# Layer 2 of a fused attention and two-layer kernel as seven products of halved operands

## The chip, the cores and the metric

The kernel runs on one core of a Trainium2 chip. The metric is the device time of one execution in microseconds, the median of the runs shown. The engines are named as in the profile: PE (TensorE, matrix products), PEld (its weight loads), DVE (VectorE), ACT (ScalarE), POOL (GpSimd) and SP (SyncE, which only issues transfers here).

## The reference

Eight batches of 8 heads, 576 positions and 64 features go through causal attention, where heads 0 to 3 see the last 32 positions ("local") and heads 4 to 7 the positions of the same residue modulo 32 ("strided"). The result, 4608 tokens by 512, goes through two layers:

```python
x = attn_out.transpose(0, 2, 1, 3).reshape(B * S, H * D)   # 4608 x 512
h = x @ w_in                                               # 4608 x 2048
g = np.maximum(h, 0.0) + alpha * np.minimum(h, 0.0)
return g @ w_out                                           # 4608 x 512
```

## The kernel before

The 4608 tokens of the two layers are nine chunks of 512. A chunk is two stages on PE, with attention for a later batch laid between their pieces.

**Layer 1** (`lin1_piece`, lines 614 to 639): 16 pieces, one for each block m of 128 columns of d_ff. A piece is four matmuls of 512 moving columns (line 624, `win16` stationary, `xT` moving) into one PSUM buffer `hps`. ACT then forms `neg` = relu(-h) (line 634), and DVE forms g = neg * (1 - alpha, negated) + h in f16 (line 637) into `gTs[n][:, m, :]`. The DVE instruction is put on a list, `late`, and issued in the next attention step, behind the instructions of that step's piece (lines 600 to 609).

**Layer 2** (`lin2_piece`, lines 643 to 671): for each of four groups of 128 tokens, four pieces of four matmuls (line 665) with a block of g as the stationary operand and 512 columns of `wout16` moving. The sixteen matmuls of a group add up in one PSUM buffer `ops`; ACT copies it to `osb` (line 670), and SP stores it (line 671). The last group of the last chunk is made in two halves of 256 columns (lines 650 to 663), so that the last store is short.

The PSUM buffers of layer 1, layer 2 and, in chunk 0, of some scores come from one pool of three (`phpool`); a buffer is given out again when its reader is done. A second pool of three (`pspool`) serves transposes, the second half of the scores and the pv products. `gT` has two buffers, `osb` three.

**Attention** is cut into pieces, in a list written out by hand (lines 537 to 592): scores of a pair of heads (PE, then exp on ACT, then the mask multiplication on POOL, lines 414 and 421), pv products (PE line 442, then a reciprocal and a multiplication on DVE, lines 449 and 451), transposes of q and k (line 239, evacuated by DVE and ACT), and the transposition of x into `xT`, on PE or by a transfer. `xT` is a ring of four batches of 576 tokens (line 50); batch b lies at (b % 4) * 576, and a chunk that runs over the end of the ring has its layer-1 matmuls split in two.

**The order.** Every engine runs its instructions in the order in which the code issues them (`keep`). The loop at lines 790 to 806 goes over chunks 1 to 8 and, in each, over 32 pieces, 16 of layer 1 and 16 of layer 2; behind each piece it issues as many attention steps as a running account gives (line 801), so that the pieces of one batch are spread over the chunk. Chunk 0 has its own loops (lines 778 to 785). POOL's queue also holds casts (`cast_copy`, line 183) and the issues of many loads (lines 114 to 171), in the same order as the pieces that they belong to. Batches 2 to 7 are computed beside chunks 1 to 6; chunks 7 and 8 have no attention beside them.

Of the kernel before, what the change touches and what calls it, by code (L numbers as in the profile page):

```python
# [31 lines left out]
def kernel(  # L32
# [24 lines left out]
    hpool = ctx.enter_context(tc.tile_pool(name="half", bufs=4))  # L57
    xpool = ctx.enter_context(tc.tile_pool(name="xp", bufs=3))
    rpool = ctx.enter_context(tc.tile_pool(name="rp", bufs=4))
    gpool = ctx.enter_context(tc.tile_pool(name="gp", bufs=2))  # L60
    npool = ctx.enter_context(tc.tile_pool(name="np", bufs=3))
    opool = ctx.enter_context(tc.tile_pool(name="op", bufs=3))
    pspool = ctx.enter_context(tc.tile_pool(name="ps", bufs=3, space=bass.MemoryType.PSUM))
    phpool = ctx.enter_context(tc.tile_pool(name="ph", bufs=3, space=bass.MemoryType.PSUM))
    pbpool = ctx.enter_context(tc.tile_pool(name="pb", bufs=1, space=bass.MemoryType.PSUM))
# [390 lines left out]
    def x_piece(P):  # L456
        xp = pspool.tile([128, 1024], F16, tag="ps", name="xp")
        for t in range(P.n):
            keep(nc.tensor.transpose(  # L459
                xp[:, P.w * t : P.w * t + P.w], P.x16[0 : P.w, 128 * t : 128 * t + 128], ident[0 : P.w, 0 : P.w]))  # L460
        base = (P.b % 4) * S
        if P.strided:
            keep(nc.scalar.copy(  # L463
                xT[:, P.hp, base : base + S].rearrange("r (p t) -> r p t", t=8),
                xp[:, 0:576].rearrange("r (t p) -> r p t", t=8)))
        else:
            cast_copy("act" if P.b < NEARLY and P.hp == 0 else "dve",
                      xT[:, P.hp, base : base + S], xp[:, 0:576])

    def x_dma(P):  # L470
        base = (P.b % 4) * S
        if P.strided:
            P.xs = xpool.tile([128, 8, 80], F16, tag="xs", bufs=2, name="xs")
            keep(nc.sync.dma_start_transpose(P.xs, P.x16[0:80, :]))
        else:
            keep(nc.sync.dma_start_transpose(
                xT[:, P.hp, base : base + S].rearrange("r (w p) -> r w p", p=96), P.x16[0:96, 0:768]))

    def x_copy(P):
        base = (P.b % 4) * S  # L480
# [116 lines left out]

        return max(i for i, (g, _) in enumerate(pieces) if g == 4 * b + 3) + 1

    late = []  # L600

    def attn_step(end):
        if pos["i"] < end:
            pieces[pos["i"]][1]()
            pos["i"] += 1
        while late:
            late.pop(0)()
        if defer:
            defer.pop(0)()


    gTs = {}

    def lin1_piece(n, m):
        if m == 0:
            gTs[n] = gpool.tile([128, 16, 512], F16, tag="gT", name="gT")
        c0 = (512 * n) % RING
        parts = [(c0, 0, min(512, RING - c0))]
        if c0 + 512 > RING:
            parts.append((0, RING - c0, 512 - (RING - c0)))  # L620
        hps = phpool.tile([128, 512], F32, tag="hps", name="hps")
        for kk in range(4):
            for x, (src, dst, w) in enumerate(parts):
                keep(nc.tensor.matmul(  # L624
                    hps[:, dst : dst + w],
                    win16[:, kk, 128 * m : 128 * m + 128],
                    xT[:, kk, src : src + w],
                    start=(kk == 0 and x == 0),
                    stop=(kk == 3 and x == len(parts) - 1),
                    skip_group_check=True,  # L630
                ))

        neg = npool.tile([128, 512], F32, tag="neg", name="neg")
        keep(nc.scalar.activation(neg, hps, AF.Relu, scale=-1.0))  # L634

        def fin():
            keep(nc.vector.scalar_tensor_tensor(  # L637
                gTs[n][:, m, :], neg, oma[:, m : m + 1], hps, op0=ALU.mult, op1=ALU.add))
        late.append(fin)

    ops_cur = {}

    def lin2_piece(n, i):
        mt, part = i // 4, i % 4
        last = n == NCH - 1
        if part == 0:
            ops_cur["t"] = phpool.tile([128, 512], F32, tag="hps", name="ops")
        ops = ops_cur["t"]
        r0 = 512 * n + 128 * mt
        if last and mt == 3:  # L650

            if part in (1, 3):
                return
            c0 = 128 * part
            half = phpool.tile([128, 512], F32, tag="hps", name="ops3") if part else ops
            for kf in range(16):
                keep(nc.tensor.matmul(  # L657
                    half[:, 0:256], gTs[n][:, kf, 128 * mt : 128 * mt + 128],
                    wout16[:, kf, c0 : c0 + 256], start=(kf == 0), stop=(kf == 15)))
            osb = opool.tile([128, 512], F32, tag="osb", name="osb")  # L660
            keep(nc.vector.tensor_copy(osb[:, 0:256], half[:, 0:256]))
            keep(nc.sync.dma_start(out[r0 : r0 + 128, c0 : c0 + 256], osb[:, 0:256]))
            return
        for kf in range(4 * part, 4 * part + 4):
            keep(nc.tensor.matmul(  # L665
                ops, gTs[n][:, kf, 128 * mt : 128 * mt + 128], wout16[:, kf, :],
                start=(kf == 0), stop=(kf == 15)))
# [169 lines left out]
```

## Time and profile before

| | |
|---|---|
| median of 3 runs | 325.08 us (324.74 to 327.92) |
| span of the profiled execution, first to last instruction | 321.1 us |
| PE, DVE, ACT, POOL busy | 312.0, 180.8, 173.0, 144.0 us |
| mean granted TensorE clock | 1.000 |
| chunk 1, from the stretch 63.9 to 99.7 | 35.8 us |
| chunk 5, from the stretch 198.5 to 231.4 | 32.9 us |
| chunk 7, from the stretch 262.2 to 289.8 | 27.6 us |

The time of the profiled execution itself is not listed beside its span; the median lies 4.0 us above the span. A profile's "busy" counts an engine as busy while an instruction runs; matmuls are pipelined, so the time that one takes from PE is read from the distance of the next one, not from its own duration. In the groups the figures after the bar are busy time in us, mean ns of one, then the idle time of the engine before them with what ended it.

### The profile page before, as it was taken

The page shows a single profiled execution, that of the slowest core. Times are in us where ns is not written, and L with a number is a line of the kernel's source. Part 1 is how long each engine was busy: PE and PEld are TensorE (multiplying, and loading weights), DVE is VectorE, ACT ScalarE, POOL GpSimd, SP SyncE. Part 2 cuts the span into 40 slices and gives each one's busy share as a digit, 9 for nine tenths or more (in the row PEclk, how much of TensorE's full clock was granted, in tenths as well). Part 3 has the DMA queues.
Part 4 walks back from the last instruction along what each step waited for, and adds up shares of the span by engine and source line. Part 5 has one row for each costly group of instructions (what it writes and reads, how often), then busy time and mean ns, then how long its engine had stood idle before and what let it go on. Part 6 is the DMA issues. An engine that isn't in the chain of part 4 may idle for free.

```text
span 321.1 us, 6319 instructions
## 1 busy us (share of the span) xinstructions
PE 312.0 (97%) x2493; PEld 162.8 (51%) x2493; DVE 180.8 (56%) x354; ACT 173.0 (54%) x322; POOL 144.0 (45%) x154
## 2 busy tenths in 40 slices
PE   6999989999999999999999999999999999999995
PEld 2564456554554454445568754455444544444444
DVE  5576836477554873388338833884288328406801
ACT  1765655368347753774477546754576157416610
POOL 8772489406998445844485338532612200000000
PEclk9999999999999999999999999999999999999999
DMA  7999999995599975997399639972611220020011
GB/s 235 194 206 207 228 174 176 182 270 159 105 141 200 200 81 127 199 149 97 91 182 202 93 88 167 84 94 62 141 51 20 61 94 2 0 98 35 0 65 65
DMA packets 77597, 40.33 MB, mean 126 GB/s; under 512 B 58480, under 2 KB 69248, under 8 KB 77568
## 3 DMA queue, kind: packets, MB, share of 16 engines
q0 software_dynamic: 41728, 17.38, 46.5%
q1 hardware_dynamic: 35840, 22.55, 29.4%
q8 instruction: 19, 0.31, 0.4%
q14 instruction: 10, 0.08, 0.1%
HBM read 38.01 MB, written 9.44 MB: 148 GB/s over the span
## 4 chain that ended last, share of the span: by engine, by line
PE 88%; DMA 4%; DVE 2%; ACT 2%; POOL 2%; issue 1%; SPq 0%; DVEq 0%; ACTq 0%
PE hps L624 38%; PE ops L665 36%; PE pv L442 4%; PE tp L239 2%; DMA xs<-x16s 2%; DMA kl<-in_k_dram 2%; PE wps L687 2%; PE sp L399 1%; PE xp L459 1%; PE ops L657 1%; ACT qT L179 1%; PE sph L399 1%; DVE qT L181 1%; POOL vs L183 1%; DVE x L451 1%
## 5 line engine op out<-in xcount | busy, mean ns | idle before, releaser
L637 DVE SCALAR_TENSOR_TENSOR gT<-neg,oma,hps 128x512 f16<-128x512 f32 x144 | 106.1, 744 | 53.1 <-ACT neg L634 45.0
L665 PE MATMUL ops<-wout,gT 128*128 128x512 f16 x560 | 135.3, 379 | 0.0
L624 PE MATMUL hps<-xT,win 128*128 128x512 f16 (+1 forms) x640 | 132.6, 358 | 0.5
L634 ACT ACTIVATE neg<-hps 128x512 f32<-128x512 f32 x144 | 86.1, 598 | 38.8 <-PE hps L624 38.8
L624 PEld LDWEIGHTS <-win 128*128 128x128 f16 x640 | 60.2, 98 | 59.4 <-issue 3.0
L665 PEld LDWEIGHTS <-gT 128*128 128x128 f16 x560 | 49.1, 98 | 47.1
L414 POOL TENSOR_TENSOR et<-et,consts 128x576 f16<-128x576 f16 (+1 forms) x24 | 30.6, 1275 | 82.1 <-ACT et L412 77.9
L670 ACT COPY osb<-ops 128x512 f32<-128x512 f32 x35 | 20.5, 586 | 66.3 <-PE ops L665 66.0
L449 DVE RECIPROCAL rc<-pv 72x6 f32<-72x6 f32 (+2 forms) x80 | 14.9, 186 | 53.5 <-PE pv L442 53.1
L451 DVE TENSOR_TENSOR x<-pv,rc 96x384 f16<-96x384 f32 (+2 forms) x62 | 33.0, 532 | 2.1
L442 PEld LDWEIGHTS <-et 72*128 72x128 f16 (+1 forms) x448 | 24.2, 98 | 16.9 <-POOL et L421 0.9
L421 POOL TENSOR_TENSOR et<-et,consts 128x576 f16<-128x576 f16 (+1 forms) x24 | 30.5, 1270 | 2.6 <-ACT et L418 2.4
L412 ACT ACTIVATE et<-sp 128x576 f16<-128x576 f32 (+1 forms) x24 | 15.5, 646 | 10.4 <-PE sp L399 10.4
L418 ACT ACTIVATE et<-sph 128x288 f16<-128x288 f32 (+1 forms) x48 | 18.6, 408 | 0.0
L687 PE MATMUL wps<-wrm 128*128 128x512 f16 x44 | 15.7, 431 | 1.2 <-DVE wrm L699 1.2
L442 PE MATMUL pv<-vs,et 72*128 72x65 f16 x256 | 15.5, 193 | 0.0
L183 POOL COPY vs<-stv 72x1024 f16<-72x1024 f16 x14 | 14.3, 1032 | 0.0
L171 POOL DMA_DIRECT2D vl<-in_v_dram x8 | 11.3, 1410 | 5.1 <-PE pv L442 4.0
L399 PEld LDWEIGHTS <-kT 64*128 64x128 f16 x336 | 7.1, 95 | 9.9 <-issue 8.9
L442 PE MATMUL pv<-vl,et 128*128 128x65 f16 x192 | 11.1, 194 | 0.4 <-POOL et L421 0.4
L181 DVE COPY qT<-tp 128x1024 f16<-128x1024 f16 (+1 forms) x9 | 9.4, 1045 | 3.3 <-PE tp L239 3.3
L463 ACT COPY xT<-xp 128x576 f16<-128x576 f16 x10 | 6.4, 639 | 6.8 <-PE xp L459 6.8
(88 smaller groups left out, 201.1 us busy)
## 6 DMA issues: line engine op xcount, KB each, us to landing
out_dram<-osb SPq DMA_DIRECT2D x35, 256.0 KB, 2.3
ql<-in_q_dram SPq DMA_DIRECT2D x6, 512.0 KB, 5.1
kl<-in_k_dram SPq DMA_DIRECT2D x6, 512.0 KB, 5.8
stv<-in_v_dram POOLq DMA_DIRECT2D x8, 288.0 KB, 7.2
vl<-in_v_dram POOLq DMA_DIRECT2D x6, 384.0 KB, 7.4
win<-in_moe_w_in_dram POOLq DMA_DIRECT2D x4, 512.0 KB, 9.6
wout<-in_moe_w_out_dram POOLq DMA_DIRECT2D x4, 512.0 KB, 13.4
qsd<-in_q_dram POOLq DMA_DIRECT2D x6, 288.0 KB, 6.9
```

Source lines behind the costliest of these rows:

```text
L183: keep(nc.gpsimd.tensor_copy(o, i))
L414: keep(nc.gpsimd.tensor_tensor(mv, mv, m, op=ALU.mult))
L418: keep(nc.scalar.activation(ev[:, n * y : n * y + n], sps[y][0:r, 0:n], AF.Exp, scale=SCALE))
L421: keep(nc.gpsimd.tensor_tensor(mv, mv, m, op=ALU.mult))
L442: keep(nc.tensor.matmul(pv[:, 65 * x : 65 * x + 65], et[0:r, c : c + 128], v16[0:r, 2 * P.pr + hh, t, :] if P.strided else v16[:, 6 * (2 * ...
L451: keep(nc.vector.tensor_tensor(P.x16[0:w, c0 : c0 + 64 * nb].rearrange("r (c e) -> r c e", e=64), pvv[:, :, 0:64], rc[0:w, 0:nb].unsqueeze ...
L624: keep(nc.tensor.matmul(hps[:, dst : dst + w], win16[:, kk, 128 * m : 128 * m + 128], xT[:, kk, src : src + w], start=(kk == 0 and x == 0) ...
L634: keep(nc.scalar.activation(neg, hps, AF.Relu, scale=-1.0))
L637: keep(nc.vector.scalar_tensor_tensor(gTs[n][:, m, :], neg, oma[:, m : m + 1], hps, op0=ALU.mult, op1=ALU.add))
L665: keep(nc.tensor.matmul(ops, gTs[n][:, kf, 128 * mt : 128 * mt + 128], wout16[:, kf, :], start=(kf == 0), stop=(kf == 15)))
L670: keep(nc.scalar.copy(osb, ops))
L687: keep(nc.tensor.matmul(wps, wrm[:, 0:128], wrm, start=True, stop=True))
```

## The change

For chunks 1 to 8, layer 2 is computed with seven products of halves instead of eight. The tokens of a chunk are two halves of 256 (`lo`, `hi`), the output columns two halves of 256, and the sixteen d_ff blocks two sets of eight, the even and the odd ones. Each product is 2 x 8 matmuls (two groups of 128 tokens, eight blocks) with 256 moving columns, accumulating in one half of a PSUM buffer.

- The products need sums of g, in a new tile `sg`. DVE forms two (`g_sums`) in three parts, behind pieces 7, 13 and 15 of layer 1 (4, 3 and 1 blocks of 256 elements); POOL forms the other two (`g_sums2`), each in two parts of 1024 elements, issued behind pieces 8 and 12 of layer 1 and behind the first and the fifth piece of layer 2.
- They need sums of the weights, made once on DVE: three sums (`wt`) in six instructions of 1024 elements beside layer 2 of chunk 0, and a fourth, in place in `wout16`, in two instructions behind pieces 2 and 5 of chunk 1's layer 1.
- The products are combined partly in PSUM and partly by DVE: five additions of 128x512 from PSUM, and two copies by ACT (P1, P2), take the place of ACT's four copies. Three PSUM buffers X, Y and V hold the products. Each chunk stores four blocks of 256 tokens by 256 columns. In the last chunk, V is two buffers, and its additions and stores are halves.
- `gT` has one buffer instead of two, `osb` five instead of three, and `xT` holds three batches instead of four, so that chunks 3 and 6 run over its end (before: chunk 4).
- `late` is gone: the g instruction is issued directly behind `neg`, ahead of the next attention piece. The 30 pieces of a chunk have their own spread of the attention steps.

```diff
-    RING = 4 * S
+    RING = 3 * S
+    FAST = 1
+    GS = {7: (0, 4), 13: (4, 7), 15: (7, 8)}
...
-    gpool = ctx.enter_context(tc.tile_pool(name="gp", bufs=2))
+    gpool = ctx.enter_context(tc.tile_pool(name="gp", bufs=1))
...
-    opool = ctx.enter_context(tc.tile_pool(name="op", bufs=3))
+    opool = ctx.enter_context(tc.tile_pool(name="op", bufs=5))
...
-        while late:
-            late.pop(0)()
...
-        def fin():
-            keep(nc.vector.scalar_tensor_tensor(
-                gTs[n][:, m, :], neg, oma[:, m : m + 1], hps, op0=ALU.mult, op1=ALU.add))
-        late.append(fin)
+        keep(nc.vector.scalar_tensor_tensor(
+            gTs[n][:, m, :], neg, oma[:, m : m + 1], hps, op0=ALU.mult, op1=ALU.add))
+        if n >= FAST:
+            g_sums(n, m)
...
+    def g_sums(n, m):
+        if m not in GS:
+            return
+        if m == min(GS):
+            sums["t"] = cpool.tile([128, 4, 8, 256], F16, tag="sg", name="sg")
+        a, b = GS[m]
+        st, g = sums["t"], gTs[n].rearrange("r (p j) t -> r j p t", j=2)
+        lo, hi = slice(0, 256), slice(256, 512)
+        P = slice(a, b)
+        sub(nc.vector, st[:, 0, P], g[:, 0, P, hi], g[:, 1, P, hi], ALU.add)
+        sub(nc.vector, st[:, 1, P], st[:, 0, P], g[:, 0, P, lo])
+
+    def g_sums2(n, P, k):
+        ...
+        if k == 2:
+            sub(nc.gpsimd, st[:, 2, P], g[:, 0, P, lo], g[:, 0, P, hi])
+        else:
+            sub(nc.gpsimd, st[:, 3, P], g[:, 1, P, lo], st[:, 1, P])
+
+    def w_sums(k, P):
+        w = wout16.rearrange("r (p j) c -> r j p c", j=2)
+        lo, hi = slice(0, 256), slice(256, 512)
+        o, x, y, op = (
+            (wt[:, 0, P], w[:, 1, P, hi], w[:, 0, P, hi], ALU.subtract),
+            (wt[:, 1, P], wt[:, 0, P], w[:, 0, P, lo], ALU.add),
+            (wt[:, 2, P], w[:, 1, P, lo], wt[:, 1, P], ALU.subtract),
+            (w[:, 0, P, hi], w[:, 0, P, hi], w[:, 0, P, lo], ALU.subtract))[k]
+        sub(nc.vector, o, x, y, op)
+
+    PRODUCTS = ("P1", "P6", "P2", "P7", "P5", "P4", "P3")
+
+    def fast_piece(n, i):
+        name, tb = PRODUCTS[i // 2], i % 2
...
+        bank, x, y = {
+            "P1": ("X", g[:, 0, :, lo], w[:, 0, :, lo]),
+            "P2": ("X", g[:, 1, :, lo], w[:, 1, :, lo]),
+            "P6": ("Y", st[:, 1], wt[:, 1]),
+            "P7": ("Y", st[:, 2], wt[:, 0]),
+            "P4": ("Y", g[:, 1, :, hi], wt[:, 2]),
+            "P5": ("V", st[:, 0], w[:, 0, :, hi]),
+            "P3": ("V", st[:, 3], w[:, 1, :, hi]),
+        }[name]
...
+        for p in range(8):
+            keep(nc.tensor.matmul(
+                z[:, 256 * tb : 256 * tb + 256], x[:, p, 128 * tb : 128 * tb + 128], y[:, p],
+                start=(opens and p == 0 and (tb == 0 or own)), stop=(ends and p == 7),
+                skip_group_check=True))
+        if tb == 0 and not own:
+            return
...
+        if name == "P1":
+            keep(nc.scalar.copy(new("21"), z))
+        elif name == "P6":
+            sub(nc.vector, new("12"), z, cur["21"], ALU.add)
+        elif name == "P2":
+            keep(nc.scalar.copy(new("11"), z))
+            store(0, 0, cur["11"])
+        elif name == "P7":
+            sub(nc.vector, new("22"), z, cur["21"], ALU.add)
+        elif name == "P5":
+            sub(nc.vector, cur["22"][:, c], z[:, c], cur["22"][:, c], ALU.add)
+            store(1, 1, cur["22"], h)
+        elif name == "P4":
+            sub(nc.vector, cur["21"], z, cur["21"], ALU.add)
+            store(1, 0, cur["21"])
+        else:
+            sub(nc.vector, cur["12"][:, c], z[:, c], cur["12"][:, c], ALU.add)
+            store(0, 1, cur["12"], h)
...
     for i in range(16):
         lin2_piece(0, i)
+        if i % 2 and i < 12:
+            w_sums(i // 4, slice(4 * (i // 2 % 2), 4 * (i // 2 % 2) + 4))
...
-        for i in range(32):
+        for i in range(30):
             if i < 16:
                 lin1_piece(n, i)
+                if n == 1 and i in (2, 5):
+                    w_sums(3, slice(0, 4) if i == 2 else slice(4, 8))
+                if i == 8:
+                    g_sums2(n, slice(0, 4), 2)
+                if i == 12:
+                    g_sums2(n, slice(0, 4), 3)
             else:
-                lin2_piece(n, i - 16)
+                fast_piece(n, i - 16)
+                if i == 16:
+                    g_sums2(n, slice(4, 8), 2)
+                if i == 20:
+                    g_sums2(n, slice(4, 8), 3)
             if i >= skip:
-                acc += left / ((21 if n == B - 2 else 22.5) - 0.5 * skip) * (0.5 if i < 16 else 1.0)
+                acc += left / ((20 if n == B - 2 else 21.2) - 0.5 * skip) * (0.5 if i < 16 else 1.0)
```

More of the change, by code (lines that the diff above doesn't have):

```diff
@@ L82 @@
     wout16 = cpool.tile([128, 16, 512], F16)
+    wt = cpool.tile([128, 3, 8, 256], F16)
     xT = cpool.tile([128, 4, RING], F16)
@@ L460, in x_piece @@
                 xp[:, P.w * t : P.w * t + P.w], P.x16[0 : P.w, 128 * t : 128 * t + 128], ident[0 : P.w, 0 : P.w]))
-        base = (P.b % 4) * S
+        base = (P.b % 3) * S
         if P.strided:
@@ L470, in x_dma @@
     def x_dma(P):
-        base = (P.b % 4) * S
+        base = (P.b % 3) * S
         if P.strided:
@@ L479, in x_copy @@
     def x_copy(P):
-        base = (P.b % 4) * S
+        base = (P.b % 3) * S
         keep(nc.scalar.copy(
@@ L598, in attn_until @@
         return max(i for i, (g, _) in enumerate(pieces) if g == 4 * b + 3) + 1
-    late = []
     def attn_step(end):
@@ L634, in lin1_piece, with sub @@
         keep(nc.scalar.activation(neg, hps, AF.Relu, scale=-1.0))
-        def fin():
-            keep(nc.vector.scalar_tensor_tensor(
-                gTs[n][:, m, :], neg, oma[:, m : m + 1], hps, op0=ALU.mult, op1=ALU.add))
-        late.append(fin)
+        keep(nc.vector.scalar_tensor_tensor(
+            gTs[n][:, m, :], neg, oma[:, m : m + 1], hps, op0=ALU.mult, op1=ALU.add))
+        if n >= FAST:
+            g_sums(n, m)
+    sums = {}
+    def sub(eng, o, x, y, op=ALU.subtract):
+        keep(eng.tensor_tensor(o, x, y, op=op))
@@ new lines, in g_sums @@
+    def g_sums(n, m):
[10 more added lines that the diff above has]
+    def g_sums2(n, P, k):
+        st, g = sums["t"], gTs[n].rearrange("r (p j) t -> r j p t", j=2)
+        lo, hi = slice(0, 256), slice(256, 512)
[3 more added lines that the diff above has]
+            sub(nc.gpsimd, st[:, 3, P], g[:, 1, P, lo], st[:, 1, P])
@@ new lines, in w_sums @@
+    def w_sums(k, P):
+        w = wout16.rearrange("r (p j) c -> r j p c", j=2)
+        lo, hi = slice(0, 256), slice(256, 512)
+        o, x, y, op = (
[5 more added lines that the diff above has]
+    PRODUCTS = ("P1", "P6", "P2", "P7", "P5", "P4", "P3")
@@ new lines, with new, store @@
+    cur = {}
+    def fast_piece(n, i):
+        name, tb = PRODUCTS[i // 2], i % 2
+        last = n == NCH - 1
+        g = gTs[n].rearrange("r (p j) t -> r j p t", j=2)
+        w = wout16.rearrange("r (p j) c -> r j p c", j=2)
+        st = sums["t"]
+        lo, hi = slice(0, 256), slice(256, 512)
+        bank, x, y = {
[7 more added lines that the diff above has]
+        }[name]
+        opens = name in ("P1", "P6", "P5")
+        ends = name in ("P2", "P4", "P3")
+        if opens and tb == 0:
+            cur[bank] = [phpool.tile([128, 512], F32, tag="hps", name="f" + bank)] * 2
+            if last and bank == "V":
+                cur[bank] = [cur[bank][0], pspool.tile([128, 512], F32, tag="ps", name="fV1")]
+        z = cur[bank][tb]
+        own = last and bank == "V"
+        for p in range(8):
[5 more added lines that the diff above has]
+            return
+        def new(key):
+            cur[key] = opool.tile([128, 512], F32, tag="osb", name="o" + key)
+            return cur[key]
+        def store(i, k, t, h=slice(0, 2)):
+            r0, m = 512 * n + 256 * i + 128 * h.start, h.stop - h.start
+            keep(nc.sync.dma_start(
+                out[r0 : r0 + 128 * m, 256 * k : 256 * k + 256].rearrange("(b p) c -> p b c", p=128),
+                t[:, 256 * h.start : 256 * h.stop].rearrange("p (b c) -> p b c", c=256)))
+        h = slice(tb, tb + 1) if own else slice(0, 2)
+        c = slice(256 * h.start, 256 * h.stop)
+        if name == "P1":
[16 more added lines that the diff above has]
+            store(0, 1, cur["12"], h)
```

## The prediction

> **What bounds the kernel now.** I read the page first for the share of each engine, then the chain of waits for what sets the end, then the stretches stage by stage, then the groups by shape for prices, and last the timelines of three places that the change touches.
>
> ```profile
> span 321.1 us, 6319 instructions
> ...
> PE 312.0 (97%) x2493; PEld 162.8 (51%) x2493; DVE 180.8 (56%) x354; ACT 173.0 (54%) x322; POOL 144.0 (45%) x154
> ```
>
> PE is busy 97% of the span. Its weight loads (PEld) lie beside its matmuls.
>
> ```profile
> 165.47 2.62 PE hps L624 x24
> ...
> 262.19 13.81 PE hps L624 x64
> 276.00 13.81 PE ops L665 x64
> ...
> 313.99 3.51 PE ops L657 x32
> ```
>
> This is the chain of waits (start, length, what). In chunk 7 PE runs 64 matmuls of 512 columns in 13.81 us, 0.216 each. The 256-column ones, each with its own weight load, take 2.62/24 = 0.109 (chunk 4, where the x ring wraps) and 3.51/32 = 0.110. Half the columns cost half the time, so a product of halves is paid by columns.
>
> ```profile
> core 0: us, PE busy (x) PEld busy (x) DVE busy (x) ACT busy (x) POOL busy (x), PEclk, DMA share, GB/s
> 63.90:99.70 35.80, 35.02 (x315) 17.85 (x314) 21.77 (x42) 22.75 (x44) 24.76 (x24) 1.00 1.00 168
> ...
> 198.50:231.40 32.90, 32.82 (x268) 16.33 (x266) 19.57 (x38) 19.26 (x36) 16.92 (x16) 1.00 0.70 108
> ...
> 262.20:276.00 13.80, 13.80 (x65) 6.25 (x64) 10.65 (x15) 9.62 (x17) 0.00 (x0) 1.00 0.05 20
> ```
>
> The stretches: chunk 1, chunk 5, and layer 1 of chunk 7. DVE's average of 56% hides that it is the near second in layer 1: 10.65 of 13.80 there, for fifteen of the sixteen g instructions.
>
> ```profile
> L637 DVE SCALAR_TENSOR_TENSOR gT<-neg,oma,hps 128x512 f16<-128x512 f32 x144 | 106.1, 744 | 53.1 <-ACT neg L634 45.0
> ...
> L451 DVE TENSOR_TENSOR x<-pv,rc 96x384 f16<-96x384 f32 x32 | 17.7, 553 | 1.1
> ...
> L414 POOL TENSOR_TENSOR et<-et,consts 128x576 f16<-128x576 f16 x12 | 15.3, 1278 | 38.5 <-ACT et L412 38.4
> ...
> L181 DVE COPY xT<-xp 128x576 f16<-128x576 f16 x2 | 0.9, 458 | 1.9 <-PE xp L459 1.9
> ```
>
> The groups by shape give the prices (mean ns of one after the bar).
>
> ```profile
> 274.08 3.34 DVE L637 SCALAR_TENSOR_TENSOR gT<-neg,oma,hps 128x512 f16<-128x512 f32 x4
> ...
> 275.84 2.97 PE L665 MATMUL ops<-wout,gT 128*128 128x512 f16 x13
> 276.04 0.60 ACT L634 ACTIVATE neg<-hps 128x512 f32<-128x512 f32 x1 [0.27 <-PE hps L624]
> ```
>
> The end of layer 1 in chunk 7: PE leaves the last piece (call its end E15) at 275.84, ACT's neg starts 0.20 later, and the last g ends at 277.42, E15 + 1.58. With three hps buffers, piece m+3 may start when g of piece m is done, Em + 1.58, and PE wants it at Em + 1.73. **The slack is 0.15 us.** Before, that is enough.
>
> **The change, part by part.** The sum is made against the profiled span of 321.1; the median of 325.08 lies 4.0 above it, and I add the change to the median.
>
> *PE.* 64 x 0.216 = 13.81 becomes 7 x 16 = 112 matmuls of 256 columns, 112 x 0.1095 = 12.26: -1.55 a chunk, -12.4 over chunks 1 to 8. All of it lies on the chain.
>
> *VectorE sums in layer 1.* Two additions each over 1024 elements (after piece 7), 768 (after 13) and 256 (after 15). No row shows an all-f16 SBUF addition. The xT copy moves two f16 a cycle (458 ns for 576 with a fixed part of about 0.15, which the x rows give: 421 for 256, 553 for 384). The other end is one a cycle (1225 for 1024 in the qT copy). The xT row is nearest in type and stride, so 0.69, 0.56 and 0.29 each; the other end would be 1.22, 0.95 and 0.42.
> In chunks 7 and 8 the first pair holds g of piece 8 back by 1.38; less the slack, PE stands 1.25 before piece 11. After piece 13 the pair of 1.11 lies ahead of g14: g14 ends at E13 + 1.58 + 1.11 + 0.75 + 0.09 = E13 + 3.53. Product P1 takes g14 as its eighth block, wanted at E13 + 1.73 + 0.77 = 2.50: 1.03 standing. The third pair ends at E15 + 3.1, and P6 wants it at E15 + 3.55: nothing, as long as nothing delays it. So 2.3 a chunk.
> In chunks 2 to 6 attention pieces lie between (pv 0.19 on PE but 0.70 on DVE, scores 0.37 on PE). Followed by hand through chunk 5 in the new order, piece 11 stands 1.5 and P1 0.8, 2.3 in all; before, layer 1 took 15.90 (198.35 to 214.25) for 15.29 of work, so 0.6 was lost already: 1.7 more. The g instruction moved ahead of the pv evacuation (no more `late`) is in this order; it frees hps earlier and pv later.
>
> *GpSimd sums.* Four of 1024 elements a chunk; by L414, 1278 x 1024/576 = 2.27 each, 9.1 a chunk. In chunks 2 to 6 POOL has gaps of 3 to 7 us (16.92 busy of 32.90), so the masks keep their times. In chunk 1 it has none:
>
> ```profile
> 74.82 1.28 POOL L414 TENSOR_TENSOR et<-et,consts 128x576 f16<-128x576 f16 x1 [11.09 <-ACT et L412]
> ...
> 78.83 1.30 POOL L421 TENSOR_TENSOR et<-et,consts 128x576 f16<-128x576 f16 x1
> ```
> ```profile
> 80.19 0.36 PE L442 MATMUL pv<-vl,et 128*128 128x65 f16 x6 [0.39 <-POOL et L421]
> ```
>
> From 74.82 POOL runs without a gap to the end of the chunk, and PE already waits for a mask at 80.19. The first sum fits into POOL's idle time before 74.82; the other three stand in the queue ahead of masks, casts and the DMA issues for the next batches (qsd, tl, stv), and push them by 3 x 2.27 = 6.8 at the end. PE had about 1 us to spare at the end (mask done at 95.80, its pv at 96.83), and part of the push meets time that PE loses on DVE anyway: chunk 1 also has the two in-place weight sums (0.69 each) in layer 1. Followed by queue, the last pv masks land near 102.7 and the chunk ends near 102.8 instead of 99.5: net 3.3, gross 4.85.
>
> *VectorE beside GpSimd.* Does a sum wait while POOL works? DVE's g instruction has one input in PSUM and keeps its 744 ns in chunks with POOL busy and idle. The nearest row for an SBUF-only DVE operation beside POOL:
>
> ```profile
> 6.02 0.19 POOL L717 MEMSET vl<- 32x64 f16 x1
> 6.04 0.98 DVE L181 CAST qs<-ql 128x1024 f16<-128x1024 f32 x1
> ...
> 7.91 0.43 DVE L181 CAST ks<-kl 128x512 f16<-128x512 f32 x1 [0.89 <-DMA kl<-in_k_dram]
> ```
>
> By the second cast 1024 elements should take 2 x 0.28 + 0.15 = 0.71; beside POOL's memsets the first took 0.98, as if it had waited. So the ends are no wait, and the rest of the POOL operation. In chunks 7 and 8 POOL is idle and starts its first sum at g6, 0.86 ahead of DVE's pair: the rest is 1.4. Its third starts at g14, just ahead of DVE's last pair, which ends at E15 + 4.65 instead of 3.1, 1.15 too late for P6. Together 2.55. In chunks 2 to 6 the same walk gives up to 3.3 when POOL is first, nothing when masks hold POOL back: I take half, 1.7. Chunk 1: up to 3, half is 1.5. I take the wait, because that cast row is the only one with both engines on SBUF alone.
> [...]
>
> *Costed at nothing, with the cover.* Five PSUM additions of 512 (0.69 each by the x rows) replace ACT's four osb copies by two in layer 2, where DVE is busy 7.35 of 17.1 us (chunk 2); without this cover each is 0.69. P2 waits for ACT's copy of P1, with P6 (1.75) between. Six weight sums in chunk 0's layer 2 fall mostly into DVE gaps of 0.5 to 3.5 us. The ring of three wraps in chunks 3 and 6 instead of 4: 64 more matmuls, +0.2. The batch overwritten in chunk n was read last in chunk n-1, so no x transfer waits. The tail keeps a half tile of 256 columns, a DVE instruction and one store. SP issues four stores a chunk as before.
>
> *Sum.* Gross: chunk 1 4.85 + 1.5; chunks 2 to 6 5 x 3.4 = 17.0; chunks 7 and 8 2 x 4.85 = 9.7; together 33.05. 33.05 - 12.4 + 0.2 = +20.9: **346.0**.
>
> **The rivals.**
> *No waits between DVE and POOL* (chance 0.28): 4.85 + 5 x 1.7 + 2 x 2.3 = 17.95; -12.4 + 0.2: +5.75, 330.8. For it: the g rows, which never lengthen. Against: the 0.98 cast.
> *The bursts are absorbed* (0.14), the other side: the PE order around pieces 8 to 11 and P1 gives DVE time to catch up, and the standing time is 1.0 a chunk in 2 to 8 and 2 in chunk 1: 9.0 - 12.2 = -3.2, 321.9. It decides where the mean gross standing time is below 12.2/8 = 1.5 a chunk. For it: pv and score pieces between. Against: chunks 7 and 8 have none, and the slack there is 0.15 against a burst of 1.38.
> *Sums at one element a cycle* (0.05): about 1.9 more a chunk, 15 in all: 346 without waits, 361 with them.
> The case forecast has 0.53, its own range 338 to 356. A measurement of this kernel can tell about 1% from no change. Faster by over 1% (below 321.8) 0.07, within 1% 0.11, slower 0.82. The range 327 to 356 leaves out most of the absorbed case and the slowest ends, 0.18.
>
> **What would show it.** Right: PE idle before L624 matmuls around piece 11 and before the P1 and P6 weight loads, ended by DVE; DVE's sums over 0.69 mean wherever POOL's sums overlap; in chunk 1 pv ended by POOL. P-matmuls at 0.11. Wrong: DVE sums at 0.69 everywhere (then 331), or layer 1 of chunk 7 still at 13.8 and its P1 without a wait (then below 325).

## The result, and the profile after

The changed kernel takes **367.19 us** (median of 4 runs, 363.65 to 371.77) against 326.5 us for the kernel before on the same chip: a ratio of 1.127, 95% interval 1.116 to 1.139. The prediction was 346.0 with a range of 327 to 356: the sign was right, the loss was about twice as large. Some executions of a kernel take several us more at a lower granted clock (the changed kernel 371.77 us at a mean of 0.958, against 363.65 at 0.972); the ratios here leave them out, so a ratio can differ from that of two medians.

The page of the changed kernel, its first lines and the granted clock in 40 slices:

```profile
span 361.9 us, 7318 instructions
...
PE 310.5 (86%) x2925; PEld 203.8 (56%) x2925; DVE 262.3 (72%) x450; ACT 165.8 (46%) x307; POOL 212.3 (59%) x186
...
PEclk9999999968699899999999999999998999999999
```

PE was 97% busy and is 86% busy: the span grew by 40.8 us, and PE stands for 51.4 us in place of 9.1. The clock row, all nines before, has holes in chunks 1, 2 and 6. The stretches, one chunk each (chunks 1, 4, 6 and 7):

```profile
core 0: us, PE busy (x) PEld busy (x) DVE busy (x) ACT busy (x) POOL busy (x), PEclk, DMA share, GB/s
63.40:110.30 46.90, 38.93 (x363) 24.61 (x362) 35.59 (x55) 21.94 (x42) 32.18 (x28) 0.85 0.76 125
...
185.30:222.70 37.40, 31.66 (x321) 20.86 (x318) 28.17 (x50) 18.39 (x34) 26.14 (x21) 1.00 0.76 128
...
259.30:296.70 37.40, 31.20 (x336) 23.89 (x333) 28.90 (x45) 14.30 (x27) 14.33 (x9) 0.95 0.26 52
296.70:327.90 31.20, 26.76 (x179) 17.10 (x178) 20.67 (x27) 11.93 (x19) 8.49 (x4) 1.00 0.10 33
```

Length of a chunk, from the first matmul of its layer 1 to that of the next:

| us | chunk 1 | 2 to 5, mean | 6 | 7 |
|---|---|---|---|---|
| before | 35.8 | 32.9 | 30.8 | 27.6 |
| changed | 46.9 | 37.2 | 37.4 | 31.2 |
| difference | +11.1 | +4.3 | +6.6 | +3.6 |
| predicted | +4.8 | +1.85 | +1.85 | +3.3 |

Chunk 7, where nothing but the two layers runs, was predicted to 0.3 us; chunk 8 grew by 2.6. The miss is in chunks 1 to 6. Who PE waits for (total us, times, longest), in the changed kernel's waits:

```profile
PE hps L624 <- DVE gT L636: 18.6, 8, 3.7
PE fX L708 <- DVE gT L636: 13.7, 8, 4.9
PE sp L403 <- DMA kT<-ksd: 4.0, 3, 1.7
PE fY L708 <- DVE sg L644: 2.7, 3, 1.2
PE sph L403 <- ACT kT L183: 2.6, 1, 2.6
```

The places are the predicted ones (piece 11, P1, P6); two waits are new, the one for the transfer of kT and, in chunk 1, the one for ACT's copy of kT. What VectorE's and GpSimd's sums cost, by groups:

```profile
L644 DVE TENSOR_TENSOR sg<-gT 128x1024 f16<-128x1024 f16 x8 | 17.3, 2157 | 0.3
...
L644 DVE TENSOR_TENSOR sg<-gT 128x768 f16<-128x768 f16 x8 | 12.0, 1497 | 0.3
...
L644 DVE TENSOR_TENSOR sg<-sg,gT 128x1024 f16<-128x1024 f16 x8 | 5.5, 692 | 0.3
L644 DVE TENSOR_TENSOR sg<-sg,gT 128x768 f16<-128x768 f16 x8 | 4.5, 558 | 0.3
```

The second sum of each pair takes 0.69 and 0.56 us, as predicted to a hundredth. The first, of the same shape, takes 2.16 and 1.50 on average: it is the one that meets a GpSimd operation. The timeline of chunk 1 and of chunk 4, an ordinary one:

```profile
84.56 2.11 POOL L644 TENSOR_TENSOR sg<-gT,sg 128x1024 f16<-128x1024 f16 x1
...
85.50 4.78 DVE L644 TENSOR_TENSOR sg<-gT 128x768 f16<-128x768 f16 x1
...
86.63 1.03 POOL L187 CAST ql<-ql 128x1024 f16<-128x1024 f32 x1
87.63 1.26 POOL L425 TENSOR_TENSOR et<-et,consts 128x576 f16<-128x576 f16 x1
88.84 1.03 POOL L187 CAST kl<-kl 128x1024 f16<-128x1024 f32 x1
...
91.59 0.40 PE L708 MATMUL fX<-wout,gT 128*128 128x256 f16 x1 [4.95 <-DVE gT L636]
...
195.62 2.12 POOL L644 TENSOR_TENSOR sg<-gT 128x1024 f16<-128x1024 f16 x1
196.34 1.94 DVE L644 TENSOR_TENSOR sg<-gT 128x1024 f16<-128x1024 f16 x1
...
200.40 1.89 PE L624 MATMUL hps<-xT,win 128*128 128x512 f16 x8 [2.55 <-DVE gT L636]
```

In chunk 4 the sum ends at 198.28, 0.54 behind the end of the GpSimd sum (197.74): it waited for the rest of that one operation. In chunk 1 it ends at 90.28, 0.41 behind the *fourth* operation. And behind long stands (2.57, 4.95, 2.56 and 3.66 us) the clock falls, to a mean of 0.50 to 0.63 in these stretches, each starting where PE goes on:

```profile
76.52:82.52 6.00, 6.00 (x26) 2.15 (x27) 2.90 (x4) 4.13 (x9) 4.42 (x5) 0.50 0.18 68
91.59:97.59 6.00, 6.00 (x68) 4.44 (x69) 4.79 (x9) 2.52 (x6) 5.97 (x5) 0.61 0.14 27
123.97:127.97 4.00, 4.00 (x26) 1.51 (x26) 2.66 (x5) 1.23 (x3) 0.94 (x1) 0.63 1.13 165
273.67:277.67 4.00, 4.00 (x21) 2.47 (x21) 2.66 (x5) 1.00 (x2) 1.48 (x1) 0.57 0.01 4
```

The clock column is the third from the right. In the first, at 0.50, eight matmuls of 512 columns take 3.39 us (79.13 to 82.52), 0.42 each in place of 0.216. What PE loses is estimated as (1 - clock) times the length: 3.0 + 2.3 + 1.5 + 1.7 = 8.5 us, in no term of the prediction.

### The profile page after: what moved, and what is told of

It is laid out like the page before. It is cut to its first block, busy times and chain, and to the rows that moved or that the text cites. A ratio compares the mean times of both kernels' runs of the same rounds, so it can differ in the third digit from the quotient of the medians.

```text
span 361.9 us, 7318 instructions
## 1 busy us (share of the span) xinstructions
PE 310.5 (86%) x2925; PEld 203.8 (56%) x2925; DVE 262.3 (72%) x450; ACT 165.8 (46%) x307; POOL 212.3 (59%) x186
## 4 chain that ended last, share of the span: by engine, by line
PE 55%; DVE 26%; DMA 9%; ACT 5%; issue 3%; SPq 0%; ACTq 0%
PE hps L624 20%; DVE sg L644 13%; PE fY L708 11%; DVE gT L636 9%; DMA kT<-ksd 8%; PE fV L708 6%; PE fX L708 4%; PE ops L770 3%; ACT neg L634 3%; PE pv L446 3%; PE sp L403 2%; PE wps L792 2%; DVE x L455 1%; PE tp L243 1%; DMA consts<-consts 1%
## 5 line engine op out<-in xcount | busy, mean ns | idle before, releaser
L624 PE MATMUL hps<-xT,win 128*128 128x512 f16 (+2 forms) x704 | 139.6, 350 | 19.5 <-DVE gT L636 18.6
L644 POOL TENSOR_TENSOR sg<-gT 128x1024 f16<-128x1024 f16 x16 | 33.9, 2121 | 66.4 <-DVE gT L636 65.9
L708 PEld LDWEIGHTS <-sg 128*128 128x128 f16 x512 | 47.6, 98 | 11.0 <-DVE sg L644 5.2
L708 PEld LDWEIGHTS <-gT 128*128 128x128 f16 x384 | 35.9, 99 | 21.7 <-DVE gT L636 16.0
L708 PE MATMUL fX<-wout,gT 128*128 128x256 f16 x256 | 34.6, 278 | 13.7 <-DVE gT L636 13.7
L644 DVE TENSOR_TENSOR sg<-gT 128x1024 f16<-128x1024 f16 (+2 forms) x24 | 39.1, 1628 | 0.8
L644 POOL TENSOR_TENSOR sg<-gT,sg 128x1024 f16<-128x1024 f16 x16 | 34.1, 2129 | 6.3 <-DVE sg L644 6.3
L708 PE MATMUL fY<-wt,sg 128*128 128x256 f16 x256 | 33.6, 276 | 3.2 <-DVE sg L644 2.7
L708 PE MATMUL fV<-wout,sg 128*128 128x256 f16 x256 | 31.9, 273 | 0.0
L644 DVE TENSOR_TENSOR o<-fY,o 128x512 f32<-128x512 f32 x24 | 16.5, 689 | 19.0 <-PE fY L708 18.5
```

The costliest lines, as they stand in the source:

```text
L624: keep(nc.tensor.matmul(hps[:, dst : dst + w], win16[:, kk, 128 * m : 128 * m + 128], xT[:, kk, src : src + w], start=(kk == 0 and x == 0) ...
L644: keep(eng.tensor_tensor(o, x, y, op=op))
L708: keep(nc.tensor.matmul(z[:, 256 * tb : 256 * tb + 256], x[:, p, 128 * tb : 128 * tb + 128], y[:, p], start=(opens and p == 0 and (tb == 0 ...
```

## The experiments

Theories at the start: **A**, VectorE's sums wait until GpSimd pauses; **B**, VectorE's bursts alone make the loss; **C**, masks and loads that stand in queues behind the new work are late.

**One part of the sums at a time.** Diffs against the changed kernel; left-out sums leave `sg` at zero (one GpSimd fill at chunk 1's start, so chunk 1 of these is not compared with the others).

```diff
     def g_sums2(n, P, k):
+        return
```
This is e1; e2 returns at once from `g_sums`, e3 from both. In e4 nothing is left out:
```diff
-            sub(nc.gpsimd, st[:, 2, P], g[:, 0, P, lo], g[:, 0, P, hi])
+            sub(nc.vector, st[:, 2, P], g[:, 0, P, lo], g[:, 0, P, hi])
...
-            sub(nc.gpsimd, st[:, 3, P], g[:, 1, P, lo], st[:, 1, P])
+            sub(nc.vector, st[:, 3, P], g[:, 1, P, lo], st[:, 1, P])
```

> The changed kernel without GpSimd's four sums (two of the four parts of sg are filled once with zeros and never renewed; all products are still made). Theory A (a VectorE sum with both inputs in SBUF waits until GpSimd pauses): in chunks 7 and 8, where GpSimd then does nothing, all sums take 0.69, 0.56 and 0.29 us and chunk 7 falls from 30.0 to about 28.4 us; in chunks 1 to 6 the masks still hold sums back; about 345 us in all. Theory B (the bursts of sums on VectorE alone hold g back, GpSimd has no part in it): chunk 7 stays at 30.0 and the time within 5 us of the changed kernel. Theory C (what costs in chunks 1 to 6 are late transposed loads and masks behind GpSimd's sums): chunks 7 and 8 stay, chunks 1 to 6 fall by about 2 us each.

> The changed kernel without VectorE's six sums of g in each chunk (two parts of sg are filled once with zeros); GpSimd's four stay. A and B: no standing of PE in layer 1, chunks 7 and 8 at 26.1 us, about 315 us in all with up to 3 us for masks behind GpSimd's sums in chunk 1. C: chunks 2 to 5 still stand about 1.5 us each at the scores that need the transposed k, and chunk 1 keeps most of its loss: about 325 us.

> The changed kernel without any sum of g (sg filled once with zeros); products, weight sums, additions after the products, ring of three and the new order stay. All theories: the product gain of 12.4 us shows nearly whole, about 314 us. If it is over 320, something else than the sums costs: the additions on VectorE, the ring of three, the missing late list or the stores.

> The changed kernel with GpSimd's four sums done by VectorE at the same places; nothing is left out. A: the sums in chunks 7 and 8 no longer wait (0.69 each), but four more bursts of 0.69 to 1.38 stand ahead of g; chunk 7 about 30, chunks 2 to 6 less than now, about 352 us in all. B: 2.8 us more VectorE work a chunk, about 385 us.

| sums of g | us | ratio to before (95%) | chunks 2 to 5 | 6 | 7 |
|---|---|---|---|---|---|
| none (e3) | 320.98 | 0.983 (0.977 to 0.989) | 32.3 | 29.3 | 26.9 |
| GpSimd's only (e2) | 325.35 | 0.981 (0.972 to 0.990) | 32.35 | 29.3 | 26.8 |
| VectorE's only (e1) | 348.21 | 1.068 (1.059 to 1.077) | 35.4 | 32.3 | 29.0 |
| all, on VectorE (e4) | 357.01 | 1.096 (1.086 to 1.106) | 36.35 | 33.4 | 29.8 |
| both (changed) | 367.19 | 1.127 (1.116 to 1.139) | 37.2 | 37.4 | 31.2 |

By the chunks, GpSimd's sums alone cost 1.1 us in chunk 1 (39.6 against 38.5) and nothing in the others, which is all that is left to C for masks behind GpSimd's sums. The 325.35 of e2 is not their price: its profiled execution was 2.65 us late before chunk 1 began, where no sum is made. VectorE's alone cost 3.1 a chunk in chunks 2 to 5, and the two together 4.9: 1.8 is what they do to each other. In the 3.1 the pair behind piece 13 meets a mask, here in chunk 3 of e1:

```profile
164.26 1.39 DVE L644 TENSOR_TENSOR sg<-gT 128x768 f16<-128x768 f16 x1
```

That is 0.8 more than the 0.56 of the second sum. So VectorE's bursts make about 2.3 of the 4.9, and 2.6 come with GpSimd: B holds for about half. The 314 us expected without any sums did not come either: PE waits 4.2 us for kT there, in chunks 2 to 5, and 2.3 for a mask in chunk 1. Giving GpSimd's share to the busier VectorE is 10 us *better* than leaving it where it was.

**The wait by itself.** In the kernel without sums, behind the last chunk, one VectorE operation becomes ready beside a chain of GpSimd operations.

```diff
+    nc.gpsimd.tensor_tensor(a, b, g0, op=ALU.add)
+    for x in range(4):
+        nc.gpsimd.tensor_tensor(o[x], g2, g3, op=ALU.add)
+    nc.vector.tensor_tensor(b, a, g1, op=ALU.add)
```

> Left out: all sums of g, as before. Added after the last chunk, where nothing else runs: six cases of one VectorE operation that becomes ready beside a chain of GpSimd operations of 1024 f16 values (2.12 us each). Theory A (the pair of inputs is kept until GpSimd pauses): VectorE's sum of two SBUF inputs takes 0.69 us alone, but 8 to 9 us when it becomes ready behind the first of five GpSimd sums in a row, and some 6 to 7 us when it becomes ready in the middle of the second; with a pause of GpSimd behind its second sum the same operation ends at that pause, after about 1 to 2 us. Theory of the prediction (the wait is the rest of one GpSimd operation): 0.7 to 2.8 us in each of these cases. An addition with one input in PSUM takes its 0.69 us in both. Open to both: a copy on VectorE (one input) beside GpSimd sums, and a sum on VectorE beside GpSimd copies: 0.3 to 0.7 us if only two inputs against two inputs wait, 8 to 9 if every GpSimd operation keeps VectorE out.

The timeline of that stretch:

```profile
317.86 0.69 DVE L951 TENSOR_TENSOR sg<-gT,sg 128x1024 f16<-128x1024 f16 x1
...
320.76 8.78 POOL L945 TENSOR_TENSOR sg<-gT 128x1024 f16<-128x1024 f16 x4
320.84 2.59 DVE L954 TENSOR_TENSOR sg<-sg,gT 128x1024 f16<-128x1024 f16 x1 [2.29 <-POOL sg L941]
...
338.11 2.32 DVE L960 COPY sg<-sg 128x1024 f16<-128x1024 f16 x1 [4.97 <-POOL sg L941]
...
349.73 1.52 DVE L964 TENSOR_TENSOR sg<-sg,gT 128x1024 f16<-128x1024 f16 x1 [9.30 <-ACT sg L963]
...
359.70 0.69 DVE L968 TENSOR_TENSOR og<-zz,of 128x512 f32<-128x512 f32 x1 [8.45 <-ACT of L967]
```

Alone 0.69; beside four GpSimd sums in a row 2.59, so it gets in after the first (0.08 into 2.12 of it, 2.04 + 0.69 = 2.73 at most); in the middle of one 1.52. A copy of 1024 values waits too (2.32; the qT copies of that size take 1.23 in the kernel before); the addition with an input in PSUM does not (0.69). **Theory A as I put it falls, and for these cases the prediction's step stands**: the wait is the rest of one operation (2.59 - 0.69 = 1.90 us, with 2.04 of the GpSimd sum left). What makes the engines wait for each other, no run shows. Two more runs looked for what differs in chunks 1 and 6.

> Left out: all sums of g inside the chunks. Added after the last chunk, where nothing else runs: seven cases of one VectorE sum of two SBUF inputs that becomes ready early in the first of several GpSimd operations in a row, with the kinds, shapes and strides that stand side by side in chunks 1 and 6: mask multiplication and sum; sum, cast of q, mask, cast, mask; masks alone; casts alone; sums alone; masks and casts in turn beside a small and a middling VectorE sum. Rest-of-one-operation theory (the six cases measured by themselves): in every case VectorE's sum ends 0.2 to 0.8 us behind the end of the operation in which it became ready, and the 4.78 us in chunk 1 and 3.58 us in chunk 6 have another cause. Rival: a change of kind, or a mask or a cast, keeps VectorE out over the boundary: the mixed cases take 3 to 5 us while the sums alone take about 2.5 us.

> Left out: all sums of g inside the chunks. Added after the last chunk: four cases of VectorE's activation (one input in PSUM) and, directly behind it, the sum of two SBUF inputs, in the shapes of chunks 1 and 6, beside GpSimd operations in a row: sum, cast, mask, cast (chunk 1's order); mask, sum, mask (chunk 6's); mask, cast, mask, cast beside the smallest sum; four masks behind two activations. Theory (a VectorE sum that follows directly behind another VectorE operation does not get in at the boundary between two GpSimd operations that are both ready): 3 to 5 us for the sums of 768 and 1024 values, while they got in at the first boundary where VectorE had been idle. Rival: 0.2 to 0.8 us behind the first boundary here as well, and the long waits of chunks 1 and 6 stay open.

Chunk 1's order in the first of the two, from its timeline:

```profile
322.59 2.11 POOL L940 TENSOR_TENSOR sg<-gT 128x1024 f16<-128x1024 f16 x1
322.90 2.22 DVE L952 TENSOR_TENSOR sg<-sg,gT 128x768 f16<-128x768 f16 x1 [2.46 <-ACT sg L937]
324.65 1.37 POOL L944 CAST sg<-fl 128x1024 f16<-128x1024 f32 x1
```

VectorE ends at 325.12, 0.42 behind the end of the sum, and the cast has to wait (1.37 against 1.03). In six cases of that run (the seventh met no GpSimd operation) and in all four of the other VectorE got in at the first boundary; directly behind an activation, chunk 1's order took 1.37. So neither the kind of the GpSimd operations nor the VectorE operation ahead explains the 4.78 of chunk 1 and the 3.58 of chunk 6. They come at the same places in other kernels: in chunk 1 4.96 with VectorE's sums alone, where masks and casts stand in a row, 4.91 with the stores held (below), and 6.67 with all sums on VectorE. In all of these, and in chunk 6, the wait ended when GpSimd had nothing more ready (in chunk 1 always at the end of the cast of `kl`), and behind the operations waited for in chunks 2 to 5 of the changed kernel GpSimd idles or issues a transfer. These rows alone would fit theory A. What speaks against it inside a kernel is e4, here in chunk 2: a sum gets in between two masks that stand back to back, and the second mask takes 1.70 in place of 1.27.

```profile
129.99 1.27 POOL L418 TENSOR_TENSOR et<-et,consts 72x576 f16<-72x576 f16 x1 [5.73 <-ACT et L416]
131.23 1.70 POOL L425 TENSOR_TENSOR et<-et,consts 72x576 f16<-72x576 f16 x1
```
```profile
130.25 1.56 DVE L644 TENSOR_TENSOR sg<-gT,sg 128x1024 f16<-128x1024 f16 x1
```

Why VectorE misses the boundaries in chunks 1 and 6 **stays open**.

**The clock.** To the kernel before, only stands are added:

```diff
+                if i == 8 and n > 1:
+                    for _ in range({2: 8, 3: 10, 4: 11, 5: 12, 6: 14, 7: 16, 8: 20}[n]):
+                        nc.vector.memset(pad, 0.0)
```

> The kernel before, with one thing added: fills of a small tile on VectorE after the ninth block of layer 1, 8, 10, 11, 12, 14, 16 and 20 of them in chunks 2 to 8 (0.25 us each by the fills at the start, so 2.0 to 5.0 us), which make PE stand. Theory (a stand of PE above some 2.5 us costs the granted clock): behind stands under about 2 us the clock stays at 1.00; behind those above 2.6 us it is 0.50 for 3 to 5 us, so the chunk loses the stand and half of that again. Rival (the clock fell in chunk 1 for another reason, the many engines that ran beside): the clock stays at 1.00 behind every stand and each chunk loses the stand alone.

The shortest stand and the third, and the clock in the 4 us behind each:

```profile
115.04 4.44 PE L624 MATMUL hps<-xT,win 128*128 128x512 f16 x12 [2.35 <-DVE gT L637]
...
191.26 4.18 PE L624 MATMUL hps<-xT,win 128*128 128x256 f16 x24 [3.50 <-DVE gT L637]
```
```profile
115.04:119.04 4.00, 4.00 (x11) 1.50 (x11) 2.99 (x6) 1.19 (x2) 0.00 (x0) 0.58 1.24 134
...
191.26:195.26 4.00, 4.00 (x24) 2.90 (x23) 2.68 (x6) 1.19 (x2) 0.00 (x0) 0.64 0.39 69
```

All seven stands (2.35 to 7.14 us) were followed by a lower clock, 0.50 to 0.64 over 4 us. The chunk with the stand of 2.35 took 37.1 us in place of 32.9: 4.2 for 2.35. The theory holds, with a lower edge than I gave. In the chunks of all traces of this study no stand up to 1.8 us lowered the clock (1.80 in e4: 1.00), every one from 2.88 up did (2.88 in e1: 0.50 in the third and fourth us behind it), and between 2.2 and 2.6 both are found: 2.27 in e2 and 2.56 in chunk 2 of the changed kernel lowered it (0.50 in the third and fourth us, and a mean of 0.63 over 4 us), 2.24 in chunk 7 and 2.56 in chunk 5 of the changed kernel left it at 1.00. What decides between them is not shown. In the first 15 us of a kernel less was enough: in e13 a stand of 1.73, close behind one of 1.44, was followed by 0.79 and 0.50.

**The transfer of kT.** In the kernel without sums PE stood 0.9 to 1.5 us for kT in each of chunks 2 to 5. On SP's queue there (first fence) two stores stand ahead of the transposes, and one waits for an addition; with the stores held until the next chunk's layer 1 (second fence) they do not:

```profile
160.78 4.31 SPq L719 DMA_DIRECT2D out_dram<-o  x2
165.63 1.52 SPq L132 DMA_TRANSPOSE qT<-qsd  x1
167.25 3.98 SPq L132 DMA_TRANSPOSE kT<-ksd  x1
```
```profile
159.05 1.34 SPq L132 DMA_TRANSPOSE qT<-qsd  x1
160.48 1.99 SPq L132 DMA_TRANSPOSE kT<-ksd  x1
```

```diff
-            keep(nc.sync.dma_start(out[...], t[...]))
+            held.append(lambda: keep(nc.sync.dma_start(out[...], t[...])))   # run after piece 3 of the next chunk
```

> The kernel without sums of g and with the stores issued in the next chunk's layer 1, once more, for its profile: the profiled execution of the first try took 783.6 us with every PE instruction three times as long. Left out: all sums of g. Theory (the stores ahead of the transposes on SP make kT late): no wait for kT of 1.5 us in chunks 2 to 5, which take about 30.7 us against 32.2 to 32.8 without the edit. Rival: the waits stay.

> The changed kernel whole, with one edit: the four stores of a chunk are issued in the next chunk's layer 1, so that on SP's queue none stands ahead of the strided transposes of q and k. Theory: the waits for kT (4.0 us in three places in the changed kernel, and 8% of its chain of waits) go, and chunks 2 to 5 shrink by about 1 us each: 363 us against 367. Rival: the transposes are late for another reason, or VectorE's sums end the chunk at the same time anyway: 367 us within 2, chunks 2 to 5 at 37.4 us as before.

Without sums: 318.09 us, 0.979 (0.972 to 0.986), no wait for kT left, and chunks 2 to 5 take 31.2 against 32.3 (a first run of the same kernel gave 320.32; one of its four executions took 783.6, with PE busy for 777 in place of 301, which stays unexplained). The edit changes the place in the queue and also takes the stores' traffic away from the transposes, whose second row falls from 3.98 to 1.99 us; the two are not told apart. In the changed kernel the same edit is worth nothing: 367.6, 1.132 (1.123 to 1.140), chunks 2 to 5 at 37.4. The waits for kT are gone there too, but the stands of 2.50 to 2.56 ahead of piece 11 in chunks 3, 4 and 5, harmless in the changed kernel (clock 1.00 behind them), now lower the clock (0.57 to 0.59 over 4 us); the stretch of chunk 4:

```profile
201.22:205.22 4.00, 4.00 (x25) 1.44 (x25) 2.67 (x5) 0.99 (x2) 0.95 (x1) 0.57 1.13 168
```

1.7 us of clock, (1 - 0.57) x 4, take the place of 1.5 us of waiting there.

**The side steps.** The kernel before with the ring of three and without `late`:

> The kernel before with two of the change's side steps alone: the x ring of three batches, and the VectorE half of the activation issued at once in place of one attention piece later. Theory: both are worth nothing, 324 to 328 us. Rival: the ring makes layer 1 wait for x at a chunk's start (0.6 us was seen at chunk 7 without sums) or the activation ahead of an attention piece takes VectorE from it: some 0.6 us in each of eight chunks, 330 us or more.

325.01 us, 0.998 (0.994 to 1.002): nothing, as predicted.

**A version out of the waits.** Four steps: all sums on VectorE at layer 2 (e8); P1, P6, P7 and P4 added up in one PSUM bank so that neighbours use different banks and two additions become ScalarE copies (e11); two rounds of moving the sums between attention's VectorE operations (e13, e16). All hold the stores, and make seven products in chunks 2 to 8 only.

```diff
-    PRODUCTS = ("P1", "P6", "P2", "P7", "P5", "P4", "P3")
+    PRODUCTS = ("P1", "P2", "P6", "P5", "P7", "P3", "P4")     # e11; banks Y X Y V Y V Y
+    SUMS = {14: [(0, A)], 15: [(1, A)], 16: [(0, Z)], 17: [(1, Z)],
+            20: [(2, A), (2, Z)], 21: [(3, A), (3, Z)]}        # e16: piece -> sums, all VectorE
```

> All sums of g on VectorE, none in layer 1 and none on GpSimd: halves of four blocks each, issued beside the products P1, P2, P6 and P7 in the order P1, P2, P6, P7, P5, P4, P3; P1's copy in two halves; the seven products in chunks 2 to 8 only; stores behind the transposes. Theory (the loss comes from layer 1's bursts, from waiting for GpSimd, and from the stores): 7 chunks x 1.55 us less on PE and some 4 us less of waits than the kernel without sums shows, against a few tenths a chunk for VectorE: 312 to 319 us. Rival: VectorE is short of time in layer 2 too (5.5 us of sums, 3.4 of additions in some 17 us, beside attention's), P6 and P7 wait for it: 325 to 332 us.

> The version that the runs point to: order P1, P2, P6, P5, P7, P3, P4, with P1, P6, P7 and P4 added up in one PSUM bank and read after each, P2 in a second, P5 and P3 in a third, so that no product follows directly in the bank that is being read; two of the five additions become copies on ScalarE. All sums of g on VectorE between the last two blocks of layer 1 and the middle of layer 2, none on GpSimd; stores behind the transposes; seven products in chunks 2 to 8 only. Theory (with sums out of layer 1, out of GpSimd's way and no read between neighbours, only the PE saving is left): chunks 3 to 6 take 31.5 to 32 us against 32.9 before, the whole 316 to 320 us. Rival: VectorE is still short in layer 2 and PE's work comes back as waits of a few tenths: 324 to 329 us.

> The products in alternating banks once more, with the two stands that its trace still shows taken away: the sums for P7 are issued three and two pieces later, so that VectorE's copies of the transposed q tail stand ahead of them (stands of 0.23, 0.28 and 0.44 us), and P4's copy goes from ScalarE to VectorE, which is free there, so that ScalarE's copy of x for the next chunk is not behind it (0.30 us). Theory: chunks 3 to 6 take 31.6 to 31.9 us against 32.5, the whole 318 to 321 us. Rival: the stands move to P6 and P7, which then wait for the sums; 324 us as before.

> The products in alternating banks a third time, with the sums for P7 and P3 issued one to three pieces earlier, right behind VectorE's copies of the transposed q tail and ahead of GpSimd's masks, beside which the two sums for P3 took 3.58 us together and made PE stand for 1.00 us in front of P3. Theory: that stand goes, chunks 3 to 5 take 32.0 us against 33.0, the whole about 318 us, 0.975 to 0.985 of before. Rival: the sums delay attention's normalisation instead, which gives the time back; 323 us.

| | us | ratio to before (95%) | chunk 4 |
|---|---|---|---|
| e8 | 331.59 | 1.022 (1.015 to 1.029) | 33.4 |
| e11 | 324.52 | 0.997 (0.993 to 1.001) | 32.5 |
| e13 | 323.24 | 0.990 (0.985 to 0.994) | 32.9 |
| e16 | 322.10 | **0.988 (0.981 to 0.996)** | 32.0 |

For e8 the rival held: PE hardly waits long (its longest listed wait in the chunks is 0.8), but layer 2 is 2.2 us longer (17.63 in chunk 4 from the first product to the next chunk, 15.41 in the kernel without sums), with PE late at P2, P6 and P7: stands of up to 0.5 us. In e13 two sums took 3.58 us beside GpSimd's masks and copies, and P3 waited 1.00. In e16 that is gone; chunk 4 of it:

```profile
169.30:201.20 31.90, 31.44 (x318) 20.94 (x315) 26.39 (x51) 18.84 (x35) 18.62 (x16) 1.00 0.92 142
```

From its first to the next chunk's first matmul it takes 32.0 against 33.0 before: of the 1.55 us of PE work, about 1.0 arrives. It beats both kernels, the one before by 1.2% (0.4 to 1.9), less than the 318 us expected. In chunks 2 to 5 its sums do not wait for GpSimd; a mask waits for them instead (2.59 us in place of 1.27 in chunk 4). The change of banks and that of the sums' places came in the same run (e11), so what each of them gave is not shown.

## Why the prediction was wrong

The places and the price of PE's work were right. What failed: the waits between VectorE and GpSimd were taken at half, 0.6 us a chunk was taken off VectorE's term that stayed lost, and two terms stood at nothing, the clock that falls behind a long stand (8.5 us) and the stores ahead of the transposes (4.0 us of waits).

- **PE, -1.55 a chunk: right.** Without sums and with the stores held, chunks 2 to 5 take 31.2 us, 1.7 less.
- **VectorE sums at 0.69 and 0.56: right**, and so were their places. The forecast's "two a cycle" and "one a cycle" are 0.53 and 1.05 ns a value in its two copy rows ((458 - 150)/576 and (1225 - 150)/1024); no trace shows how long a cycle is. For the stands of 1.5 and 0.8 that the walk gave, chunk 5 with VectorE's sums alone shows 1.31 and 1.47, with the 0.8 of the mask in the second. **The step "0.6 was lost already: 1.7 more" failed**: the chunks 2 to 5 grow by 3.1. The new stands do not take the place of the 0.6. Without sums and with the stores held, layer 1 of chunk 5 takes 15.8 us (15.9 before), and with VectorE's sums alone it takes 16.0 beside its stands and the wait for kT.
- **GpSimd sums at 2.27: right in size** (2.12), **wrong in effect.** The gross 4.85 for chunk 1's GpSimd queue did not come: in e2 GpSimd's sums add 1.1 there, and the changed kernel has no wait of PE for a mask in that chunk.
- **VectorE beside GpSimd: the wait right, the step "half of 3.3" failed.** That the wait is the rest of the other's operation was the author's estimate from one cast (0.98 in place of 0.71, beside memsets); the cases by themselves show it (2.59 and 1.52 in place of 0.69). I halved the waits in chunks 2 to 6 because masks might hold GpSimd back. They do not: in chunks 2 to 5 the first sum of each pair waited every time (1.94, 1.38 and 0.97 in place of 0.69, 0.56 and 0.29: 2.75 us a chunk; in chunk time 2.6 by the experiments, in place of 1.7). For chunk 1 the "half of 3" became 4.22 for one sum, and in chunk 6 2.89 for one; these two are longer than the rest of one operation, and open.
- **Missing: what else stands in VectorE's queue behind a sum.** In chunk 1 it is the copy of the transposed q tail. ACT's copy of k comes behind it, and the scores behind that:

```profile
73.25 2.06 DVE L644 TENSOR_TENSOR sg<-gT 128x1024 f16<-128x1024 f16 x1
75.34 0.69 DVE L644 TENSOR_TENSOR sg<-sg,gT 128x1024 f16<-128x1024 f16 x1
75.95 0.22 DVE L185 COPY qT<-tt 128x128 f16<-128x128 f16 x1
```
```profile
76.20 0.27 ACT L183 COPY kT<-tt 128x128 f16<-128x128 f16 x1 [3.74 <-DVE qT L185]
```
```profile
76.52 0.26 PE L403 MATMUL sph<-qT,kT 64*128 64x96 f16 x2 [2.57 <-ACT kT L183]
```

- **Missing: the clock.** 8.5 us, over a third of the 20 us (40.8 - 20.9) by which the span missed. Chunk 1 adds up: 34.25 (35.8 - 1.55) + stands of 0.27, 2.57 and 4.95 + 5.3 of clock = 47.3; it took 46.9.
- **"SP issues four stores a chunk as before": failed** as a step costed at nothing. Four they are, but one now waits for an addition with the transposes behind it: 4.0 us of waits for kT in chunks 3 to 5. Its removal alone gave nothing back.
- **Chunks 7 and 8: right in sum, in part by luck.** They grew by 3.6 and 2.6 for the 3.3 forecast. The three stands came at the places that the walk gave, but in chunk 7 they are 2.24, 0.82 and 0.75, 3.8 in place of 4.85, and a wait of 0.62 for xT stands beside them that the sum did not have.

By chunks the miss is 6.3 us in chunk 1, 2.45 in each of chunks 2 to 5 and 4.75 in chunk 6; chunks 7 and 8 together took 0.4 less than forecast. In chunks 2 to 5 the 2.45 are 0.95 that PE's gain lacks even without sums (32.3 in place of 31.35, with waits for kT of 0.9 to 1.5), 1.4 in VectorE's sums alone (the 0.6 and the wait for a mask) and 0.1 in what the two do to each other. The 8.5 us of clock and the 4.0 of waits for kT lie in these; the terms overlap, as the stores show, so they are not gains to be had one by one.

## What to carry to other kernels

Where an engine's wait can be "the rest of the other's operation", take the whole wait (1.9 us for a sum of 0.69 in the case by itself) at every meeting and look for an order in which they do not meet; here the seven products in other banks, one chunk fewer, with all sums on VectorE ahead of GpSimd's masks and with the stores held, were 45 us faster than the changed kernel (322.1 against 367.2), while the PE work saved is about 11. Price a stand of PE above about 2.2 us (2.27 was the shortest in the chunks that lowered the clock here) with what its clock may lose behind it, about 1.5 to 3 us more here. When a step moves a store, read what is queued behind it.

## What was not expected of the hardware

- A stand of PE of 2.35 us was enough to lower the granted clock for about 4 us (0.66 and 0.50 in the two stretches of 2 us behind it), and one of 2.57 for 6 us (0.50); one of 2.55 left it at 1.00 in the changed kernel, and in the same place with the stores held it was 0.57 over 4 us.
- A VectorE copy of f16 from SBUF to SBUF beside GpSimd's sums took 2.32 us, so it waited with one input alone; an addition with an input in PSUM did not (0.69).
- GpSimd is held up as well: its cast of 1.03 us took 1.37, and in the last version its mask of 1.27 us took 2.59, when VectorE got in ahead of it.
